# Where 1e-9 is added to the softmax sums: VectorE or ScalarE, in a block-sparse attention with a gated projection

## The chip, the cores and the metric

One core of a Trainium2 chip runs the whole program. The metric is the device time of one execution in microseconds (us), the median of several runs. In the text PE is TensorE (matmuls; PEld its weight loads), DVE is VectorE, ACT is ScalarE, POOL is GpSimd and SP is SyncE, which here only issues transfers.

## The reference

Block-sparse attention over 4 batches, 8 heads, 768 positions and 64 columns per head, in blocks of 32 positions. A query block sees itself and its two neighbours, the first and the last block, and three drawn blocks; the first and the last query block see everything. The result goes through a gated projection: a causal convolution over 5 positions gives a gate, and two 512x512 matrices frame it.

```python
    scores = np.where(mask, scores, -1000000000.0)
    scores = scores - np.max(scores, axis=-1, keepdims=True)
    attn = np.exp(scores)
    attn = attn / (np.sum(attn, axis=-1, keepdims=True) + 1e-09)
    return np.matmul(attn, v).astype(np.float32)
...
    gate = 1.0 / (1.0 + np.exp(-gate_pre))
    val = x @ w_val
    return (gate * val @ w_out).astype(np.float32)
```

The `1e-09` in the fourth line is what the change is about.

## The kernel before

The four batches are worked in two phases of two batches each (`ph.f` is 0 or 1). A phase has 22 ordinary query blocks, each one unit of work for both batches and all heads, and two global blocks (first and last query block of one batch), each two units. So a phase has 24 parts (`pr`), and the value sums of each part end in one small tile `rs`.

The loop at the end of `attention_moe` runs over steps n and writes down, for several units at once, what each engine does, in a pipeline: in step n PE computes the scores `sc` of unit n, then the value products `av` of unit n-2, then the transposes `pt` of the weights of unit n-1. DVE takes the row maxima `mx` of unit n, ACT computes the exponentials `pe` of unit n (four instructions, two for each half), then copies the transposed weights `ptr` of unit n-1 out of PSUM. PE needs `ptr` for the next `av`.

Normalisation is three steps, all in `values`, all on DVE: the sums (column D of `av`, four per partition) plus 1e-9 go to `rs`, a reciprocal of `rs` in place, and the product of `av` and `rs` into `x`. The last two are put into the list `drip` and written out a little later, usually one DVE instruction after the addition; between them stands an instruction of other work. A step later DVE transposes `x` into `xT`, from which the gates and the projection are computed.

During the first phase DVE has further work in between. The eight 128-row pieces of the two weight matrices come as 64-bit numbers and are decoded by four DVE instructions each (`words` and `wst` in the trace), a cast on ACT (`wv` or `wo`) and a subtraction on DVE for the low part. When all are decoded, the convolutions (`th`), and then the projection (`vp`, `op`) on PE, fill the steps. POOL meanwhile gathers the drawn value blocks (`vb`) and copies the drawn key blocks into place (`kg<-k`) in the first phase.

The order on every engine is fixed: the class `InOrder` chains each engine's instructions in the order in which the program names them. So an instruction that waits holds everything behind it on its engine. Nearly every instruction has line 90, that class's call; the names of the tiles tell the instructions apart.

Of the kernel before, what the change touches and what calls it, by code (L numbers as in the profile page):

```python
# [11 lines left out]
AF = mybir.ActivationFunctionType  # L12
# [4 lines left out]
B, H, S, D = 4, 8, 768, 64  # L17
# [54 lines left out]
def attention_moe(ctx, tc, qb, kb, v, sampled, w_val, conv_w, w_out, ident_in, slot_in, out):  # L72
# [29 lines left out]
    pe, dve, act, pool, sp = (InOrder(e) for e in (nc.tensor, nc.vector, nc.scalar, nc.gpsimd, nc.sync))  # L102
# [207 lines left out]
    for ph in phases:  # L310
# [3 lines left out]
        for place, i in enumerate(order):  # L314
            pr = Part()
# [198 lines left out]
    def values(un):  # L514
        pr = un.pr
        if un.end == 0:
            spare = not pr.glob and pr.ph.f == 0 and units.index(un) % 2 and units.index(un) < SPARE_UNTIL
            space, tag = (ps_moe, "mo") if spare else (ps_av, "av")
            pr.av = space.tile([128, 2, 2, DV], F32, tag=tag, name="av")
        if pr.glob:  # L520
            for h in range(2):
                for c in range(6):
                    pt = un.PT[4 * h + c if c < 4 else 4 + 2 * h + c]
                    for hp in range(HP):
                        cols = slice(BLK * hp, BLK * hp + BLK)
                        hd = 2 * hp + h
                        matmul(
                            pr.av[cols, un.end, h, :], pt[:, cols], pr.ph.vn[c][:, pr.e, hd * DV : (hd + 1) * DV],
                            start=c == 0, stop=c == 5, tile_position=(0, BLK * hp),
                        )  # L530
        else:
            products = [(c, e, h) for c in range(2) for e in range(E) for h in range(2)]
            for c, e, h in products:
                vt = (pr.vb if c else pr.va)[:, e, :]
                for hp in range(HP):
                    cols = slice(BLK * hp, BLK * hp + BLK)
                    hd = (2 * hp + h) * DV
                    matmul(
                        pr.av[cols, e, h, :], un.PT[4 * h + 2 * e + c][:, cols], vt[:, hd : hd + DV],
                        start=c + e + h == 0, stop=c + e + h == 3, tile_position=(0, BLK * hp),  # L540
                    )
        if un.last:
            rs = three.tile([128, 2, 2, 2], F32, tag="rs", name="rs")
            dve.tensor_scalar_add(rs[:, 0], pr.av[:, :, :, D], 1e-9)
            drip.append(lambda: dve.reciprocal(rs[:, 1], rs[:, 0]))
            pr.x = two.tile([128, 2, 2, D], F32, tag="x", name="x")
            drip.append(
                lambda: dve.tensor_tensor(
                    out=pr.x, in0=pr.av[:, :, :, 0:D], in1=rs[:, 1, :, :, None].to_broadcast([128, 2, 2, D]), op=ALU.mult
                )  # L550
            )
# [252 lines left out]
    for n in range(N + LAG_V):  # L804
# [36 lines left out]
        if 0 <= n - LAG_V < N:  # L841
            values(units[n - LAG_V])
# [88 lines left out]
```

## Time and profile before

| | |
|---|---|
| median of 3 runs | 354.56 us (352.15 to 356.95) |
| the profiled execution | 353.03 us, of which 351.3 us are the span in the trace |
| PE busy | 329.3 us, 94% |
| DVE busy | 274.9 us, 78% |
| ACT busy | 226.3 us, 64% |
| POOL busy | 118.7 us, 34% |

The shares are means over very different stretches. Up to some 37 us the global units run and keys arrive; up to some 98 us the weights are decoded; from 118 us on, PE has attention and projection to do side by side; the last 50 us are projection alone. The granted TensorE clock is 0.995 of full speed over the span.

### The profile page before, as it was taken

The page shows a single profiled execution, that of the slowest core. Times are in us where ns is not written, and L with a number is a line of the kernel's source. Part 1 is how long each engine was busy: PE and PEld are TensorE (multiplying, and loading weights), DVE is VectorE, ACT ScalarE, POOL GpSimd, SP SyncE. Part 2 cuts the span into 40 slices and gives each one's busy share as a digit, 9 for nine tenths or more (in the row PEclk, how much of TensorE's full clock was granted, in tenths as well). Part 3 has the DMA queues.
Part 4 walks back from the last instruction along what each step waited for, and adds up shares of the span by engine and source line. Part 5 has one row for each costly group of instructions (what it writes and reads, how often), then busy time and mean ns, then how long its engine had stood idle before and what let it go on. Part 6 is the DMA issues. An engine that isn't in the chain of part 4 may idle for free.

```text
span 351.3 us, 15356 instructions
## 1 busy us (share of the span) xinstructions
PE 329.3 (94%) x6522; PEld 258.0 (73%) x6522; DVE 274.9 (78%) x644; ACT 226.3 (64%) x505; POOL 118.7 (34%) x186
## 2 busy tenths in 40 slices
PE   8787989989867999999999999999999999999995
PEld 7465756655545887797788777887778878989894
DVE  0664878999999789759997984768987599989440
ACT  2365877687896757756785674758766786564421
POOL 1647788877643304414431222321242100000000
PEclk9899999999999999999999999999999999999999
DMA  6958587876999999774888567538663011020202
GB/s 219 395 194 261 174 266 256 276 251 170 277 283 294 385 247 305 250 225 154 273 228 279 165 205 219 173 107 251 200 204 95 12 58 62 30 90 2 90 0 90
DMA packets 47603, 67.74 MB, mean 193 GB/s; under 512 B 4400, under 2 KB 31536, under 8 KB 47536
## 3 DMA queue, kind: packets, MB, share of 16 engines
q1 hardware_dynamic: 40624, 43.10, 39.5%
q0 software_dynamic: 6336, 23.43, 21.1%
q8 instruction: 51, 0.84, 1.0%
q10 hardware_dynamic: 576, 0.24, 0.2%
q14 instruction: 16, 0.13, 0.1%
HBM read 60.46 MB, written 6.29 MB: 190 GB/s over the span
## 4 chain that ended last, share of the span: by engine, by line
PE 75%; DVE 14%; ACT 7%; issue 3%; POOL 0%; ACTq 0%; POOLq 0%; DVEq 0%
PE op L90 19%; PE vp L90 19%; PE av L90 12%; PE pt L90 11%; PE sc L90 9%; DVE mx L90 5%; PE s L90 3%; DVE words L90 3%; ACT ptr L90 3%; PE idle L90 2%; ACT pe L90 2%; DVE wst L90 2%; DVE xT L90 1%; DVE x L90 1%; DVE wv L90 1%
## 5 line engine op out<-in xcount | busy, mean ns | idle before, releaser
L90 ACT ACTIVATE pe<-sc,mx 128x256 f32<-128x256 f32 x176 | 69.1, 475 | 36.6 <-DVE mx L90 36.2
L90 POOL DMA_INDIRECT vb<-in_v,idx x44 | 44.4, 1010 | 142.7 <-PE av L90 120.8
L90 DVE SCALAR_TENSOR_TENSOR th<-xT,cw,th 128x384 f32<-128x384 f32 x128 | 79.7, 652 | 1.5 <-ACT th L90 1.5
L90 DVE TENSOR_REDUCE mx<-sc 128x2 f32<-128x512 f32 x88 | 56.3, 679 | 21.2 <-PE sc L90 17.5
L90 ACT COPY ptr<-pt 128x512 f32<-128x512 f32 x108 | 61.3, 606 | 9.3 <-PE pt L90 8.0
L90 POOL COPY kg<-k 128x256 f32 (+1 forms) x99 | 55.2, 596 | 7.5 <-PE sc L90 7.0
L90 PE MATMUL sc<-kg,qc 64*32 64x256 f32 x1408 | 53.3, 382 | 2.3 <-issue 1.1
L90 PE MATMUL op<-wo,yh 128*128 128x512 f32 x192 | 53.3, 399 | 0.0
L90 PE MATMUL pt<-ident,pe 128*128 128x128 f32 x352 | 50.4, 279 | 1.8 <-issue 1.8
L90 PE MATMUL vp<-xh,wv 128*128 128x384 f32 x256 | 51.1, 341 | 0.0
L90 PEld LDWEIGHTS vp<-xh,wv 128*128 128x128 f32 x256 | 44.3, 188 | 0.3
L90 PEld LDWEIGHTS pt<-ident,pe 128*128 128x128 f32 x352 | 38.5, 140 | 7.3 <-issue 1.9
L90 PEld LDWEIGHTS op<-wo,yh 128*128 128x128 f32 x192 | 35.3, 188 | 7.3
L90 PEld LDWEIGHTS sc<-kg,qc 64*32 64x32 f32 x1408 | 22.8, 106 | 21.2 <-issue 9.6
L90 ACT CAST yh<-y 128x384 fp32r<-128x384 f32 x32 | 16.8, 524 | 23.0 <-DVE y L90 23.0
L90 PE MATMUL av<-vb,ptr 128*32 128x65 f32 x1408 | 28.8, 220 | 2.4 <-issue 2.4
L90 PE MATMUL op<-wo,yl 128*128 128x512 f32 x96 | 30.9, 403 | 0.0
L90 PEld LDWEIGHTS av<-vn,ptr 128*32 128x32 f32 x1216 | 19.2, 109 | 14.6 <-ACT ptr L90 7.5
L90 PEld LDWEIGHTS av<-va,ptr 128*32 128x32 f32 x960 | 15.6, 109 | 17.2 <-ACT ptr L90 9.5
L90 PE MATMUL av<-vn,ptr 128*32 128x65 f32 x1216 | 24.5, 222 | 3.6 <-ACT ptr L90 1.7
L90 PE MATMUL vp<-xl,wv 128*128 128x384 f32 x128 | 27.7, 338 | 0.0
L90 DVE TENSOR_TENSOR yl<-y,yh 128x384 fp32r<-128x384 f32 x32 | 18.3, 572 | 11.4 <-ACT yh L90 11.1
(74 smaller groups left out, 421.8 us busy)
## 6 DMA issues: line engine op xcount, KB each, us to landing
kg<-in_k SPq DMA_DIRECT2D x80, 128.0 KB
qc<-in_q SPq DMA_DIRECT2D x48, 128.0 KB
k<-in_k SPq DMA_DIRECT2D x12, 512.0 KB
out<-ot SPq DMA_DIRECT2D x23, 256.0 KB
vn<-in_v SPq DMA_DIRECT2D x16, 260.0 KB
vn<-in_v SPq DMA_DIRECT2D x6, 520.0 KB
va<-in_v SPq DMA_DIRECT2D x8, 260.0 KB
wst<-in_w_val SPq DMA_DIRECT2D x8, 256.0 KB
```

Of the source, the lines that this page charges most:

```text
L90: made = getattr(self.eng, name)(*args, **kwargs)
```

## The change

The addition is made by ACT, as a copy activation with a bias of 1e-9, when the part belongs to the first phase (24 parts), and by DVE as before in the second phase (24 parts). The reciprocal and the product stay on DVE.

```diff
         if un.last:
             rs = three.tile([128, 2, 2, 2], F32, tag="rs", name="rs")
-            dve.tensor_scalar_add(rs[:, 0], pr.av[:, :, :, D], 1e-9)
+            if pr.ph.f:
+                dve.tensor_scalar_add(rs[:, 0], pr.av[:, :, :, D], 1e-9)
+            else:
+                act.activation(rs[:, 0], pr.av[:, :, :, D], AF.Copy, bias=1e-9)
             drip.append(lambda: dve.reciprocal(rs[:, 1], rs[:, 0]))
```

On DVE, in a step of the weight decoding (`mx` are the row maxima of the step's unit, `xT` the transposed output of an earlier one), the difference is this:

```order
 L90 SCALAR_TENSOR_TENSOR words<-words,wst 128x512
 L90 TENSOR_REDUCE mx<-sc 128x2 x2
-L90 TENSOR_SCALAR rs<-av 128x4
 L90 STREAM_TRANSPOSE xT<-x 128x8x32
 L90 RECIPROCAL rs<-rs 128x4
```

The addition is gone; the reciprocal keeps its place, one instruction behind the maxima.

On ACT, in the same steps, the difference is this (`wv` is a cast of decoded weights, `qc` scales the queries):

```order
 L90 CAST wv_115<-words 128x512
 L90 ACTIVATE qc<-qc 128x256
 L90 ACTIVATE pe<-sc,mx 128x256 x4
+L90 ACTIVATE rs<-av 128x4
 L90 COPY ptr<-pt 128x512 x2
 L90 CAST wv_115<-words 128x512
 L90 ACTIVATE qc<-qc 128x256
 L90 ACTIVATE pe<-sc,mx 128x256 x4
```

The addition stands behind all four exponentials of the step's unit and ahead of the two copies `ptr`.

The waits of the changed kernel at that place on DVE (in brackets the semaphores that an instruction waits on):

```order
L90 TENSOR_REDUCE mx<-sc 128x2 [waits PE_49] x2
L90 STREAM_TRANSPOSE xT<-x 128x8x32
L90 RECIPROCAL rs<-rs 128x4 [waits Activation_49]
L90 TENSOR_TENSOR x<-av,rs 128x256 [waits DVE_49,PE_49]
L90 TENSOR_REDUCE mx<-sc 128x2 [waits PE_49] x2
```

The reciprocal now waits for ACT, where it waited for DVE's own addition. The orders of PE, POOL and SP are the same in both kernels.

## Rows read from the trace of the kernel before

**Rows 1.** Stretch, length, busy us PE, PEld, DVE, ACT, POOL; clock, DMA share, GB/s
```profile
57.00:98.00 41.00, 36.67 (x1019) 23.99 (x1007) 40.69 (x88) 31.87 (x77) 31.54 (x51) 1.00 0.82 243
98.00:118.00 20.00, 15.60 (x398) 11.71 (x399) 19.85 (x48) 14.91 (x37) 8.07 (x9) 1.00 1.03 316
118.00:300.00 182.00, 181.19 (x3683) 145.87 (x3682) 149.25 (x361) 125.19 (x278) 44.05 (x50) 1.00 0.63 191
```
**Rows 2.** Chain of work that ended last, 74.4 to 74.9 us: start, us, what
```profile
74.43 0.07 DVE rs L90
...
74.83 0.09 DVE rs L90
```
**Rows 3.** Order of time on DVE: start us, us, instruction, [idle before it <-releaser]
```profile
42.18 0.17 DVE L90 RECIPROCAL rs<-rs 128x4 f32<-128x4 f32 x1
...
46.83 1.29 DVE L90 TENSOR_REDUCE mx<-sc 128x2 f32<-128x512 f32 x2 [0.86 <-PE sc L90]
...
71.31 0.12 DVE L90 RECIPROCAL rs<-rs 128x4 f32<-128x4 f32 x1
...
73.16 1.27 DVE L90 TENSOR_REDUCE mx<-sc 128x2 f32<-128x512 f32 x2
...
74.75 0.17 DVE L90 RECIPROCAL rs<-rs 128x4 f32<-128x4 f32 x1
...
78.84 1.40 DVE L90 TENSOR_SCALAR words<-wst 128x512 f32<-128x512 f32 x1
...
80.15 0.17 DVE L90 RECIPROCAL rs<-rs 128x4 f32<-128x4 f32 x1
...
102.02 0.16 DVE L90 RECIPROCAL rs<-rs 128x4 f32<-128x4 f32 x1
```
**Rows 4.** Order of time on ACT, same columns
```profile
42.48 1.09 ACT L90 COPY ptr<-pt 128x512 f32<-128x512 f32 x2
...
72.06 1.09 ACT L90 COPY ptr<-pt 128x512 f32<-128x512 f32 x2
...
73.87 1.57 ACT L90 ACTIVATE pe<-sc,mx 128x256 f32<-128x256 f32 x4 [0.40 <-DVE mx L90]
75.31 1.09 ACT L90 COPY ptr<-pt 128x512 f32<-128x512 f32 x2
...
79.72 1.09 ACT L90 COPY ptr<-pt 128x512 f32<-128x512 f32 x2
...
102.38 1.09 ACT L90 COPY ptr<-pt 128x512 f32<-128x512 f32 x2
```
**Rows 5.** Small instructions, by shape, whole span: count, busy us, mean ns, idle before
```profile
L90 DVE TENSOR_SCALAR rs<-av 128x4 f32<-128x4 f32 x48 | 7.2, 150 | 2.1 <-PE av L90 2.0
...
L90 ACT CAST cwp<-words 128x20 fp32r<-128x20 f32 x1 | 0.2, 232 | 0.0
L90 ACT ACTIVATE warm<-warm 128x1 f32<-128x1 f32 x1 | 0.2, 203 | 0.0
```
**Rows 6.** DVE by shape, 57 to 98 us: count, busy us, mean ns
```profile
L90 DVE SCALAR_TENSOR_TENSOR words<-words,wst 128x512 int32<-128x512 int32 x5 | 5.5, 1095 | 0.0
...
L90 DVE TENSOR_SCALAR words<-wst 128x512 f32<-128x512 f32 x5 | 3.6, 730 | 0.0
```
**Rows 7.** Tile words, 36 to 118 us, on DVE: ns min/median/max, first and last start
```profile
L90 DVE TENSOR_SCALAR words<-wst x8: 428/578/1398, 38.2 to 106.5; 128x512 f32<-128x512 f32 x8
L90 DVE SCALAR_TENSOR_TENSOR words<-words,wst x8: 644/766/1876, 43.0 to 111.4; 128x512 int32<-128x512 int32 x8
```
**Rows 8.** Order of time on POOL, columns as in rows 3
```profile
75.67 1.09 POOL L90 COPY kg<-k 128x256 f32 x3
...
78.73 2.91 POOL L90 COPY kg<-k 128x512 f32<-128x512 f32 x5
```
**Rows 9.** Order of time on PE, columns as in rows 3
```profile
106.30 1.09 PE L90 MATMUL pt<-ident,pe 128*128 128x128 f32 x8 [1.77 <-issue]
...
112.61 1.05 PE L90 MATMUL sc<-kg,qc 64*32 64x256 f32 x19 [0.89 <-issue]
```

## The prediction

> **What bounds the kernel now.** The page alone says PE, 94% busy. I read busy time by stretch first, because the change touches the first phase only. From 118 to 300 us PE is busy 181.19 of 182 us: what arrives there late is late at the end, since no idle time is left to take it up [rows 1]. From 57 to 98 us it is otherwise: DVE is busy 40.69 of 41 us while PE, ACT and POOL have gaps, and from 98 to 118 us DVE is again busy 19.85 of 20 us [rows 1]. The chain of waits agrees: in the decoding it runs along DVE, and `rs` appears in it twice a step, as addition at 74.43 us and as reciprocal at 74.83 [rows 2]. After 118 us DVE has gaps again, 149.25 us busy of 182 [rows 1]. So the kernel has a DVE-bound stretch up to about 108 us and a PE-bound one behind it. A microsecond added to DVE's queue in the first costs about a microsecond at the end. One added behind 118 us falls into DVE's gaps.
>
> **What is removed.** Each addition lasts 150 ns [rows 5], but its successor starts before it has ended: on the chain it holds 0.07 us [rows 2]. For the 16 additions between 37 and 104 us that is some 1.1 us saved, if nothing else happened.
>
> **What is added, on ACT.** No row shows an activation of 128x4 from PSUM. The nearest are 203 ns for 128x1 and 232 ns for 128x20 [rows 5]; the addition itself took 150 ns on DVE, which is the lower bound, and 0.30 us is the upper bound I give for the unknown read of PSUM and the signal. I take 0.25 us from its start to the moment when DVE may go on, a little above the row of 20 columns. ACT itself is busy 31.87 of 41 us [rows 1] and waits for the maxima at most steps (0.40 us before 73.87 [rows 4]), so 24 short instructions hide there; they put `ptr` off by a fraction of those 0.25 us.
>
> The Trainium skill (ScalarE: Activation LUTs, Rules for kernel authors) speaks against the change: adds belong on VectorE. The same page gives 186 ns plus 0.833 ns an element with an immediate bias; by that the addition would be 0.19 us, an estimate, and each of the 13 waits below 0.06 us shorter, 0.8 us in all. The rows of 203 and 232 ns are near it; no run shows this instruction.
>
> **The new wait.** This is the main term. DVE's reciprocal has to wait for ACT's addition, and that stands behind all four exponentials. In the step of 73.16 us the maxima start at 73.16, the exponentials at 73.87, and ACT is free for its next instruction at 75.31, where `ptr` starts now [rows 3, 4]. So the sums plus 1e-9 are there at 75.31 + 0.25 = 75.56. The reciprocal starts at 74.75 now [rows 3] and would, without the addition ahead of it, be ready at 74.68. DVE stands still for 0.88 us, and all that is queued behind it (the decoding, `x`, the next maxima, and through those the next exponentials) stands with it.
>
> I worked this out for each of the 16 steps whose maxima start between 36 and 101 us, in the same way: start of `ptr` + 0.25 - (start of the reciprocal - 0.07). The first wait that counts is 42.48 + 0.25 - 42.11 = 0.62, the longest 72.06 + 0.25 - 71.24 = 1.07, the last 102.38 + 0.25 - 101.95 = 0.68 [rows 3, 4]. In one step there is none: at 78.84 a `words` instruction of 1.40 us stands before the reciprocal, which comes at 80.15, after ACT is through at 79.72 + 0.25 [rows 3, 4]. Where DVE idles afterwards for PE, the wait is swallowed: 0.86 us before 46.83 [rows 3], and 0.5 to 0.6 us each at two other steps up to 56 us, read alike. In order, net of those gaps: 0, 0.62, 0.20, 0, 0.22, 0.47, 0.61, 0.64, 1.07, 0.88, 0, 0.86, 1.01, 0.63, 0.49, 0.68. The sum is 8.4 us; the 1.1 us saved are inside it, through the 0.07. With 0.15 us for the addition it would be 1.3 us less (13 waits of 0.10), with 0.30 us 0.7 us more.
>
> From 105 us on I count nothing, though two more steps would wait 0.7 us each: PE has waits of its own there that DVE doesn't end (0.89 us before 112.61 [rows 9]), and from 118 us it sets the pace.
>
> **What takes part of it back.** DVE's decoding instructions are slowed while POOL copies. `words` takes 0.644 us at its fastest and 1.876 at its slowest, and the long ones lie beside POOL's copies (78.84 to 80.24 on DVE against 78.73 to 81.64 on POOL) [rows 3, 7, 8]. Between 57 and 98 us five of these cost 1.095 us each on average, so 2.3 us above the fastest, and the five `words` of the other kind 0.730 against 0.428 us, 1.5 us more [rows 6, 7]; the same sum over the other decoding and gate instructions of that stretch gives another 2.7 us, 6.5 us in all. A DVE that waits for ACT is not in POOL's way: copies that fall into the wait slow nobody. POOL's copies start a fixed while after ACT's `ptr`, and so, with every wait, earlier against DVE's queue. Nothing in the trace prices this; the bounds are 0 and all 6.5 us. A group of three copies (1.09 us [rows 8]) fits into a wait of 0.9 us almost wholly, a group of five (2.91 us) outlasts it. I take 2.5 us, under half, since the groups alternate.
>
> **The sum.** 8.4 - 2.5 = 5.9 us. Against the profiled execution, 353.03 us, that is 358.9 us. The median of the runs is 354.56 us, 1.5 us above it; the forecast for a median is 354.56 + 5.9 = 360.5 us, 1.7% slower. About 2% (7.1 us, 361.65 us) is what a measurement of this kernel can tell from no change.
>
> **The rivals.**
>
> *The waits in full, slower by over 2%.* If the slowing beside POOL only moves to the instructions behind the wait, nothing comes back: 8.4 us, 363.0 us; with 0.30 us for the addition and the two waits behind 105 us on the path too it is up to 10.5 us, 365 us. For it: POOL's five-copy groups are longer than any wait. It decides once less than 1.3 us comes back. Against it: the copies do move forward against DVE by the length of the wait.
>
> *The slowing goes almost wholly, not slower.* With 6.5 us back, 8.4 - 6.5 = 1.9 us remain, 356.5 us; PE's own waits of 1.77 and 0.89 us [rows 9], which have nothing to wait for in the trace, could shrink when PE comes to them later, which brings it to 354.56. It decides from some 6 us back. The Trainium skill (SBUF — State Buffer, SBUF: two separate sides) calls the port pair that DVE and GpSimd share an exclusive lock, held for a whole instruction by whoever started first. The slowest `words`, 1.2 us above the fastest, fits that. By that rule a DVE that stands still gives the lock away, which supports some relief but not its size.
>
> *The wait isn't there, faster.* If ACT had the sums ready before DVE asks, 16 times 0.07, 1.1 us, would be saved: 353.4 us. It needs ACT to finish 0.5 to 1.1 us earlier than the rows say; only the step of 80.15 us gives that. A gain of over 2% would need all of the 6.5 us as well.
>
> **How the numbers follow.** The forecast with part taken back (4 to 8 us, 358.5 to 362.5) gets 0.45; the waits in full 0.27; the slowing almost wholly gone (0 to 4 us) 0.20; the wait hidden 0.08. The range leaves out the ends of the first and the last: 355.0 to 364.5 us. Slower by over 2% are the full waits and the upper fifth of the forecast: 0.27 + 0.09 = 0.36. Faster by over 2%: 0.03. Within 2%: 0.61.
>
> **What would show it.** In the changed profile DVE should have idle time before the reciprocal of the first phase, ended by ACT's `rs`, 9 to 11 us in all at 0.5 to 1.1 us each, and none in the second phase. ACT's `rs<-av` should last 0.2 to 0.3 us. The windows of DVE's decoding should end some 6 us later, and the time from there to the end should be as now. The mean of `words<-words,wst` should fall below 1.095 us if the slowing recedes. Wrong would be the whole argument if the idle time before the reciprocal is under 3 us; wrong in its size, if the idle time is there but PE reaches its full stretch no later, or if `words` hasn't become shorter.

## The result, and the profile after

| | before | after |
|---|---|---|
| median of 19 runs each | 352.86 us | 357.81 us |
| ratio | | 1.0146, 95% interval 1.0122 to 1.0169 |
| the profiled execution, and its span | 353.03, 351.3 us | 357.66, 355.9 us |

The change makes the kernel 1.5% slower, 5.0 us between the medians, where 5.9 us were forecast. The waits of DVE in the changed kernel (engine and tile waited for: us in total, times, longest us) have a line that the kernel before doesn't have:

```profile
DVE rs L90 <- ACT rs L90: 12.2, 19, 1.0
```

All 19 waits lie in the first phase. In order of time on DVE (columns as in [rows 3]), this is the step that [rows 3] show at 73.16 us, 0.6 us later here:

```profile
73.77 1.28 DVE L90 TENSOR_REDUCE mx<-sc 128x2 f32<-128x512 f32 x2
74.96 0.42 DVE L90 TENSOR_SCALAR wst<-wst 128x512 uint32<-128x512 uint32 x1
76.15 0.18 DVE L90 RECIPROCAL rs<-rs 128x4 f32<-128x4 f32 x1 [0.77 <-ACT rs L90]
```

and on ACT:

```profile
74.48 1.57 ACT L90 ACTIVATE pe<-sc,mx 128x256 f32<-128x256 f32 x4 [0.81 <-DVE mx L90]
75.92 0.19 ACT L90 ACTIVATE rs<-av 128x4 f32<-128x4 f32 x1
75.98 1.10 ACT L90 COPY ptr<-pt 128x512 f32<-128x512 f32 x2
```

The reciprocal starts 0.23 us after ACT has begun the addition, and the addition begins only when the four exponentials are issued. Before, the reciprocal came 1.59 us after the maxima [rows 3]; now it comes 2.38 us after them. The chain of waits, which in [rows 2] ran along DVE, now goes over to ACT and back in this step (start, us, what):

```profile
73.85 0.61 DVE mx L90
74.46 0.02 issue
74.48 0.62 ACT pe L90 x2
...
75.57 0.48 ACT pe L90
76.05 0.07 ACT rs L90
76.12 0.02 issue
76.15 0.18 DVE rs L90
```

The next views compare equal pieces of work: from the maxima of the second ordinary unit to those of the eighteenth, which is the stretch of the 16 steps in the prediction (columns as in [rows 1]: length, then busy us of PE, PEld, DVE, ACT, POOL). Before:

```profile
36.77:105.26 68.49, 59.19 (x1760) 40.16 (x1748) 64.59 (x145) 54.25 (x131) 49.87 (x78) 1.00 0.80 241
```

After:

```profile
35.09:108.91 73.82, 62.51 (x1761) 41.53 (x1757) 63.07 (x130) 55.01 (x145) 47.36 (x76) 0.98 0.76 228
```

The stretch is 73.82 - 68.49 = 5.33 us longer. DVE is busy 1.52 us less and idle 6.85 us more (10.75 against 3.90). The granted clock is 1.00 before and 0.98 after: from 103.60 us on it is 0.50, the level of 1.2 GHz, for 3.41 us; PE had just stood idle for 2.09 us. That falls into the last of the 16 steps, which grew by 1.15 us; over the other 15, at a clock of 1.00 in both (36.77 to 100.22 and 35.09 to 102.72 us), the stretch is 67.63 - 63.45 = 4.18 us longer. The start of the stretch, 1.68 us earlier in this execution, lies between 35.09 and 36.99 us in the profiles of this case, and is 36.75 us in a kernel below in which ACT makes the addition too, so I don't count it as the change's; with the 10 us up to the first projection (-0.16 us) and the rest (+1.1 us) the pieces make up the 4.6 us between the spans: -1.68 + 5.33 - 0.16 + 1.1.

### The profile page after: what moved, and what is told of

Its sections match the earlier page's. It is cut to its first block, busy times and chain, and to the rows that moved or that the text cites. A ratio compares the mean times of both kernels' runs of the same rounds, so it can differ in the third digit from the quotient of the medians.

```text
span 355.9 us, 15370 instructions
## 1 busy us (share of the span) xinstructions
PE 330.9 (93%) x6522; PEld 257.8 (72%) x6522; DVE 274.5 (77%) x620; ACT 227.8 (64%) x529; POOL 117.8 (33%) x186
## 4 chain that ended last, share of the span: by engine, by line
PE 67%; DVE 13%; ACT 11%; issue 4%; DMA 3%; SPq 0%; ACTq 0%; DVEq 0%
PE op L90 18%; PE vp L90 17%; PE av L90 11%; PE pt L90 10%; PE sc L90 8%; ACT pe L90 6%; DVE mx L90 5%; ACT ptr L90 3%; PE s L90 2%; DMA sb<-in_sampled 2%; DVE th L90 2%; DVE x L90 1%; DVE words L90 1%; DVE xT L90 1%; DMA qc<-in_q 1%
## 5 line engine op out<-in xcount | busy, mean ns | idle before, releaser
L90 PE MATMUL sc<-kg,qc 64*32 64x256 f32 x1408 | 56.7, 384 | 3.2 <-ACT pe L90 2.4
L90 PE MATMUL pt<-ident,pe 128*128 128x128 f32 x352 | 51.2, 283 | 0.0
L90 PEld LDWEIGHTS sc<-kg,qc 64*32 64x32 f32 x1408 | 23.6, 106 | 24.2 <-issue 9.3
L90 PE MATMUL av<-vb,ptr 128*32 128x65 f32 x1408 | 29.8, 221 | 4.1 <-issue 3.9
L90 PE MATMUL av<-vn,ptr 128*32 128x65 f32 x1216 | 23.5, 222 | 5.2 <-ACT ptr L90 3.5
L90 PEld LDWEIGHTS av<-va,ptr 128*32 128x32 f32 x960 | 15.5, 109 | 16.9 <-ACT ptr L90 10.3
L90 PEld LDWEIGHTS av<-vb,ptr 128*32 128x32 f32 x1408 | 24.0, 110 | 4.8 <-issue 4.8
```

Of the source, the lines that this page charges most:

```text
L90: made = getattr(self.eng, name)(*args, **kwargs)
```

## The experiments

Two theories stood against each other. The first is the prediction's: DVE waits for the place that the addition has in ACT's queue, and pays where DVE sets the pace. The rival is that the work or the signals as such cost, 24 instructions on ACT or 24 crossings between engines. Each kernel was timed against the kernel before on the same chip.

| kernel | ratio to before | 95% interval | DVE's waits for ACT's addition |
|---|---|---|---|
| the change | 1.0146 | 1.0122 to 1.0169 | 12.2 us |
| second phase instead of first | 1.0057 | 1.0023 to 1.0091 | 8.8 us |
| addition between the exponentials | 1.0008 | 0.9982 to 1.0035 | 3.2 us |
| ACT's work, nobody waits at the reciprocal | 1.0009 | 0.9981 to 1.0038 | none there |
| the wait alone | 1.0139 | 1.0082 to 1.0195 | 9.9 us |
| addition one instruction later | 1.0472 | 1.0412 to 1.0532 | 24.7 us |
| reciprocal one turn later | 1.0057 | 1.0020 to 1.0093 | 3.7 us |

### The work without the wait, and the wait without the saving

> The kernel before, with the 24 additions of the first phase made on VectorE as before and a second time on ScalarE, into a tile that nothing reads. ScalarE has the work of the change, and nobody waits for it. Theory of the wait: within 0.5 us of before. Rival (ScalarE's occupancy delays the copies of the transposed weights): 2 to 5 us above before.

```diff
             dve.tensor_scalar_add(rs[:, 0], pr.av[:, :, :, D], 1e-9)
+            if not pr.ph.f:
+                spare = three.tile([128, 2, 2], F32, tag="rx", name="rx")
+                act.activation(spare, pr.av[:, :, :, D], AF.Copy, bias=1e-9)
```

Measured 1.0009: ACT has the 24 instructions and the time stays. One flaw: `x` on DVE, behind the reciprocal, was found to wait for ACT's reading of `av`, 2.6 us in five places, so "nobody waits" is true of the reciprocal only.

> The kernel before with VectorE's 24 additions of the first phase kept, and the same 24 activations on ScalarE as in the run with extra additions, but written into the half of rs that the reciprocal overwrites, so that the reciprocal must wait for ScalarE. Against the run with extra additions only the wait is new. Theory of the wait: VectorE waits 11 to 13 us before the reciprocals, and the time is that of the change plus the VectorE slots that the change saves (1 us), 1.4 to 2.0% above before. Rival (the loss comes from something else that the change does, such as the slot taken out or the timing of the sums): within 0.5% of before.

```diff
             dve.tensor_scalar_add(rs[:, 0], pr.av[:, :, :, D], 1e-9)
+            if not pr.ph.f:
+                act.activation(rs[:, 1], pr.av[:, :, :, D], AF.Copy, bias=1e-9)
```

Measured 1.0139. This kernel differs from the one above in where ACT writes, and so in one thing: the reciprocal waits for it. Its waits:

```profile
DVE rs L90 <- ACT rs L90: 9.9, 18, 0.9
```

DVE keeps its additions here, so nothing that the change takes from DVE is needed for the loss. The wait alone brings it: the interval, 0.8 to 2.0% above before, holds the change's 1.5%. The waits are 9.9 us where 11 to 13 were expected. With these two the rival falls as far as it puts the cost on ACT's work or on the slot taken out. The crossings between engines are answered by the next kernel, which has all 24 of them.

### The place in ACT's queue

> As the change, but in the first phase the second pair of exponentials is written out behind the addition: ScalarE does two exponentials, the addition, two exponentials. VectorE's and PE's orders are those of the change. Theory of the wait: each wait before the reciprocal shrinks by the two exponentials, about 0.72 us, so from 12.2 us in all to 1 to 3 us, and the time comes back to between 1 us under and 1 us over before. Rival (the extra ScalarE work or the signal is what costs): 4 to 5 us above before, as the change.

```diff
-            if not (n and units[n - LAG_T].pr.glob and units[n - LAG_T].pr.ph.f == 0):
+            early = not (n and units[n - LAG_T].pr.glob and units[n - LAG_T].pr.ph.f == 0)
+            if early and units[n].pr.ph.f:
                 run(second_half)
...
             values(units[n - LAG_V])
+        if n < N and early:
+            run(second_half)
```

Measured 1.0008: the loss is gone, with the same instructions on each engine and the same 24 crossings as in the change. DVE's waits are 3.2 us, where 1 to 3 were expected. In order of time on ACT the addition now stands between the pairs:

```profile
73.99 0.84 ACT L90 ACTIVATE pe<-sc,mx 128x256 f32<-128x256 f32 x2 [0.34 <-DVE mx L90]
74.72 0.18 ACT L90 ACTIVATE rs<-av 128x4 f32<-128x4 f32 x1
74.78 0.85 ACT L90 ACTIVATE pe<-sc,mx 128x256 f32<-128x256 f32 x2
```

and DVE's reciprocal of that step, at 1.64 us behind its maxima, doesn't wait:

```profile
73.29 1.27 DVE L90 TENSOR_REDUCE mx<-sc 128x2 f32<-128x512 f32 x2
...
74.93 0.18 DVE L90 RECIPROCAL rs<-rs 128x4 f32<-128x4 f32 x1
```

> As the change, but ScalarE makes the addition one instruction later, between the two copies of the transposed weights. The work of every engine is that of the change. Theory of the wait: the addition comes about 0.49 us later in each step, so VectorE waits some 7 us more in the 16 steps of the decoding; the gaps on VectorE that swallowed part of the first waits are used up, so 5 to 8 us come on top of the change, 2.8 to 3.8% above before. Rival (occupancy or signals): as the change, 1.2 to 1.7% above before.

```diff
-                act.activation(rs[:, 0], pr.av[:, :, :, D], AF.Copy, bias=1e-9)
+                owns.append(lambda: act.activation(rs[:, 0], pr.av[:, :, :, D], AF.Copy, bias=1e-9))
```

Measured 1.0472: the direction of the theory, and more than its size. The waits doubled, to 24.7 us where some 19 were expected. Besides the 0.49 us, two loops show. The copy of `ptr` now ahead of the addition waits for PE at times, and DVE with it; on ACT and DVE, the longest wait:

```profile
71.63 0.59 ACT L90 COPY ptr<-pt 128x512 f32<-128x512 f32 x1 [0.70 <-PE pt L90]
...
72.11 0.18 ACT L90 ACTIVATE rs<-av 128x4 f32<-128x4 f32 x1
...
72.32 0.18 DVE L90 RECIPROCAL rs<-rs 128x4 f32<-128x4 f32 x1 [2.07 <-ACT rs L90]
```

And PE comes to wait for `x`, because the sums `av` have a single buffer in PSUM at these units, and `x` is its last reader:

```profile
114.32 0.67 PE L90 MATMUL av<-va,ptr 128*32 128x65 f32 x32 [1.33 <-DVE x L90]
...
125.53 0.67 PE L90 MATMUL av<-vn,ptr 128*32 128x65 f32 x32 [1.40 <-DVE x L90]
```

In the profile the first projection starts at 127.43 us against 115.50 before, 11.9 us; 5.7 us more come behind it, of which PE's waits between 130 and 165 us explain 3.6. The last two of those waits, 1.71 us before 162.15 and 0.97 us before 164.21, are followed by a stretch at half the clock (columns as in [rows 1]):

```profile
163.90:167.31 3.41, 3.10 (x70) 2.96 (x71) 2.62 (x8) 1.57 (x4) 0.84 (x1) 0.50 0.73 193
```

The kernel before has a clock of 1.00 all the way behind its first projection. PE is busy 3.10 us there, so the lower clock costs at most half of that, some 1.5 us; the rest, 0.6 us or more, stays open.

### The consumer's place

> As the change, with ScalarE's order untouched, but in the first phase VectorE's reciprocal is written out one turn later, so that in most decoding steps two instructions of other work stand ahead of it instead of one. Theory of the wait: VectorE has something to do while ScalarE finishes, the waits fall from 12.2 us to 3 to 5 us (in some steps there is nothing else to put ahead), and the time is 0 to 0.8% above before. Rival (the place of the addition among ScalarE's exponentials isn't the cause): as the change, 1.2 to 1.7% above.

```diff
+            if not pr.ph.f:
+                drip.append(lambda: None)
             drip.append(lambda: dve.reciprocal(rs[:, 1], rs[:, 0]))
```

Measured 1.0057, inside the expected 0 to 0.8%; the waits fall as expected:

```profile
DVE rs L90 <- ACT rs L90: 3.7, 8, 0.7
```

Another 1.2 us before two reciprocals are put down to "issue", so it may be up to 4.9 us. ACT's queue is that of the change, so moving the consumer takes away more than half of the loss.

### The other phase

> The addition moves to ScalarE in the second phase only (24 parts), and stays on VectorE in the first. Theory of the wait (VectorE's reciprocal waits for ScalarE, and that costs only where VectorE sets the pace): VectorE waits some 10 us in all in the second phase, but PE is the bound there, so the time is 0 to 1.5 us above that of before. Rival (24 more instructions on ScalarE, or 24 signals between engines, cost a fixed amount each wherever they stand): about 5 us above before, as with the change itself.

```diff
-            if pr.ph.f:
+            if not pr.ph.f:
                 dve.tensor_scalar_add(rs[:, 0], pr.av[:, :, :, D], 1e-9)
```

Measured 1.0057, 2.0 us: much less than the first phase's loss, though a little more than the 0 to 1.5 us expected. DVE waits 8.8 us on ACT's addition and 2.9 us more that the trace puts down to "issue":

```profile
DVE rs L90 <- ACT rs L90: 8.8, 12, 1.1
```

Most of that falls into DVE's gaps. Part of what is paid shows on PE, which waits for `x` as above in three places, two of them (0.84 us before 179.36, 0.54 us before 257.79) in the second phase:

```profile
PE av L90 <- DVE x L90: 1.6, 3, 0.8
```

The two come to 1.4 of some 2 us; the rest isn't traced. So the claim that DVE's gaps behind 118 us take up everything was too simple: the single buffer ties PE to DVE there too.

### What GpSimd's copies give back

> The kernel before, with GpSimd's copies of the drawn key blocks in the first phase left out (the places are set to one once at the start). VectorE's decoding is then hardly slowed by GpSimd. Together with the next run it tests whether part of the waits was paid back because GpSimd's copies fall into them. Expected: the stretch of the decoding shorter, 2 to 6 us under before.

> The change, with the same copies left out. If the waits had been paid back in part by less slowing beside GpSimd (the prediction's 2.5 us), nothing is paid back here, and the difference to the run without copies before it is 7 to 8.4 us, clearly more than the 5 us of the change. If little was paid back (as the busy times of the two profiles say, 0.4 us), the difference is again 4.5 to 6 us.

```diff
+    for t in kg:
+        pool.memset(t[:, 1:3, 0:NR], 1.0)
...
-        numbers = {eng: list(block_numbers(pr, eng)) for eng in (POOL, ACT)}
+        numbers = {POOL: [], ACT: []}
```

Measured 0.9940 (0.9895 to 0.9984) without copies before, 2.1 us under and so within the 2 to 6 expected, and 1.0056 (1.0021 to 1.0092) without copies after. They are 1.2% apart, some 4.1 us: the same as the change within the intervals, a little under the 4.5 to 6 us expected if little was paid back, and not the 2.0 to 2.4% that would follow if the copies had been paying 2.5 us back. The windows say it more sharply. The 16 steps without copies, before:

```profile
36.83:102.34 65.51, 58.14 (x1736) 40.47 (x1728) 60.42 (x145) 54.53 (x131) 28.20 (x33) 0.98 0.85 250
```

and after:

```profile
35.40:106.10 70.70, 61.03 (x1766) 41.45 (x1759) 58.75 (x129) 55.28 (x147) 28.65 (x34) 1.00 0.80 239
```

That is 70.70 - 65.51 = 5.19 us longer, DVE 1.67 us less busy and 6.86 us more idle. With the copies it was 5.33, 1.52 and 6.85 us. The clock doesn't make the difference: it is 0.98 before and 1.00 after here, and the other way round with the copies. Over the first 15 steps, at 1.00 in all four kernels, the change costs 4.18 us with the copies and 5.07 without (36.83 to 96.83 and 35.40 to 100.47 us), but DVE's busy time falls alike, by 1.63 and 1.62 us, so the 0.9 us between them is idle time.

The copies do slow DVE (64.59 against 60.42 us busy, 4.2 us), and by as much with the change (63.07 against 58.75, 4.3 us). One profile of each kernel settles this to a microsecond or so: in the four kernels with copies here in which DVE has the same 145 instructions in the 16 steps, it is busy 62.97 to 65.18 us. The two kernels of the next section, which lack the addition and its wait, have 62.29 and 62.88 us, and the change with its 9.2 us of waits has 63.07: no relief of 2.5 us shows there either.

### The addition's own worth

> The kernel before without the addition in the first phase: the reciprocal reads the sums straight from PSUM, so 1e-9 is left out there. VectorE has 24 instructions fewer and no new wait. Prices what the change saves on VectorE by itself: 16 times 0.07 us in the stretch where VectorE sets the pace, 1.1 us under before. If the slot of the addition is worth its whole 150 ns: 2.4 us under. If the waits hid a larger saving: more than 3 us under.

```diff
-            dve.tensor_scalar_add(rs[:, 0], pr.av[:, :, :, D], 1e-9)
-            drip.append(lambda: dve.reciprocal(rs[:, 1], rs[:, 0]))
+            if pr.ph.f:
+                dve.tensor_scalar_add(rs[:, 0], pr.av[:, :, :, D], 1e-9)
+                drip.append(lambda: dve.reciprocal(rs[:, 1], rs[:, 0]))
+            else:
+                drip.append(lambda: dve.reciprocal(rs[:, 1], pr.av[:, :, :, D]))
```

Measured 0.9965 (0.9934 to 0.9997), 1.2 us: what was expected of 16 slots, with an interval that nearly reaches 1.

> The kernel before without any addition, in both phases: every reciprocal reads the sums from PSUM (1e-9 is left out; each sum holds exp(0) = 1, and in fp32 1 + 1e-9 is 1). In the first phase that gained 1.2 us. In the second PE sets the pace, so the 24 further slots bring 0 to 0.5 us: 0.3 to 0.6% under before. If VectorE's slots were worth the same in both phases: 0.7 to 0.9% under.

The edit takes the same two lines out in both phases. Measured 0.9998 (0.9964 to 1.0033). Neither 0.3% nor 0.9% under can be read from it, and as it contains the kernel above, that one's 0.35% isn't settled either. By the lower end of that interval the addition on DVE costs at most 1.3 us of the whole. In the 16 steps DVE is 2.3 and 1.7 us less busy in these two kernels than before, but the stretch is 67.79 and 68.63 us long, against 68.49: most of what DVE is spared turns into idle time. No kernel here that does all the work is shown to beat the kernel before.

## Why the prediction was right, and by which steps

**The forecast.** 5.9 us, 1.7% slower; measured 1.46%, 5.0 us between the medians, and 4.6 us between the two spans. Of the 2.7 us between the forecast median, 360.5 us, and the measured 357.81, 1.7 are the median before, which came out at 352.86 and not at 354.56. The wait and its place were right. That the size came so close is luck: it came out through three errors that nearly cancel.

**What bounds the kernel: right.** DVE's queue in the decoding sets the pace; 5.33 us arise between the maxima of the second and the eighteenth ordinary unit, and PE carries them to the end. The last five waits, 3.0 us behind the 16 steps, were rightly left out: the way to the first projection is no longer for them, and they cost at most the 1.1 us by which the rest is longer.

**The addition on ACT: right in kind, about 0.03 us too dear.** From its start to the start of the reciprocal that waits for it pass 0.22 or 0.23 us, against 0.25 taken. The instruction itself lasts 0.191 us in the median, just under the 0.2 to 0.3 named as a sign. The Trainium skill (ScalarE: Activation LUTs, What ACT_TABLE_LOAD costs) gives 186 ns plus 0.833 ns an element, an estimate of 0.189 us for the instruction; the trace agrees. But the prediction took the 0.06 us between that and 0.25 off each wait, and a wait ends some 0.03 us after the instruction. That ACT hides the work was right too: 1.0009 with the work alone.

**The waits: right mechanism, a term of 8.4 us where 6.85 were.** The 16 steps hold 9.2 us of waits, against 10.3 reckoned before gaps. They aren't the reckoned ones step by step: in the steps of 60.18 and 87.32 us a decoding instruction beside POOL's copies took 1.69 and 1.49 us and covered the wait, and in the step of 78.27 us, where the rows before had such a cover [rows 3], it was gone and DVE waited 0.58 us. Of the 9.2 us, gaps swallowed 9.2 - 6.85 = 2.35, where 1.9 were reckoned.

**The saving: a mistake in the sum.** The text says that the 1.1 us saved are inside the 8.4 "through the 0.07". They aren't. Each wait was counted from the earlier time at which the reciprocal is ready; what the step grows by is that wait less the 0.07. The 1.1 us had to be taken off. DVE's busy time fell by 1.52 us with the copies and 1.67 without, which agrees with 1.1 within the spread of these profiles.

**The 2.5 us taken back: wrong.** This is the step that failed outright. DVE was not measurably less slowed by POOL for these waits: without copies the loss is the same. The sign that the prediction named, a shorter mean of `words`, was there and misled. By shape, 57 to 98 us of the kernel before and 57 to 100 us of the changed one (columns as in [rows 6]):

```profile
L90 DVE SCALAR_TENSOR_TENSOR wst<-wst 128x512 int32<-128x512 int32 x5 | 3.9, 770 | 0.0
...
L90 DVE TENSOR_TENSOR wo<-words,wo 128x512 fp32r<-128x512 f32 x2 | 1.8, 901 | 0.0
```

```profile
L90 DVE SCALAR_TENSOR_TENSOR wst<-wst 128x512 int32<-128x512 int32 x5 | 4.5, 909 | 0.0
...
L90 DVE SCALAR_TENSOR_TENSOR words<-words,wst 128x512 int32<-128x512 int32 x5 | 3.7, 735 | 0.0
...
L90 DVE TENSOR_TENSOR wo<-words,wo 128x512 fp32r<-128x512 f32 x2 | 2.3, 1174 | 0.0
```

The mean of that kind of `words` fell from 1.095 [rows 6] to 0.735 us, 1.8 us over five of them, while `wst` rose from 0.770 to 0.909 and `wo` from 0.901 to 1.174 us, together 1.2 us more: most of the collisions moved to other instructions. One shape's mean says nothing of the sum; the busy time of the stretch does.

**Added up.** Forecast: 8.4 + 0 - 2.5 = 5.9. Measured in the 16 steps: 6.85 - 1.52 + 0 = 5.33.

**The rivals.** "The waits in full" had the right mechanism, in that nothing measurable came back from POOL, and the prediction gave it less than the branch with part taken back. Its size (8.4 us and more) failed on the forgotten saving and the swallowed gaps. "The wait isn't there" failed: the reciprocal waits in 14 of the 16 steps. "The slowing goes almost wholly" failed with the runs without copies.

## What to carry to other kernels

Before moving a small instruction to an idle engine, look at where it will stand in that engine's queue and when its consumer asks: an engine with a third of its time free can still be late by four instructions at the very moment that counts. The same instruction cost nothing when it stood two exponentials earlier, and more than half of the loss went when the consumer stood one instruction later. When a forecast nets two large terms, look for the view that shows each by itself (here busy and idle time of one engine over equal work), since the total can come out right with both wrong.

## What the runs showed that I had not expected

What POOL's copies cost DVE did not fall with the change: 4.2 us in the 16 steps in the kernel before and 4.3 us in the changed one, although the two queues stand differently against each other. With longer waits some of it may come back, as the prediction had thought. In the kernel with the addition one instruction later, DVE stands still for twice as long, and is busy 60.31 us in the 16 steps, 2.8 us less than in the change with the same instructions (columns as in [rows 1]):

```profile
36.66:116.41 79.75, 63.58 (x1760) 43.27 (x1752) 60.31 (x129) 55.62 (x147) 46.06 (x78) 0.96 0.72 213
```

That is one profile, and no run tests it. And a wait of DVE reaches PE by a way that the profile before doesn't show: with one PSUM buffer for `av`, a late `x` holds PE's next products, 0.92 us once in the changed kernel (at 117.09 us), 1.4 us in two places where the additions of the second phase moved, and up to 1.40 us at a time where the addition was made later still.
